# Attention and two gated layers on one core: single accumulation banks, scores by head, another split of the first layer's blocks

## The chip, the cores and the metric

One NeuronCore of one Trainium2 chip runs the whole kernel. The metric is the device time of one execution in microseconds (us). The engines are TensorE (PE in the profile, with its weight loads as PEld), VectorE (DVE), ScalarE (ACT), GpSimd (POOL) and SyncE (SP), which issues the transfers.

## The reference

```python
def _attn_ref(q, k, v, M_prev, z_prev, beta):        # B, H, S, D = 4, 8, 576, 64
    scores = scale * np.matmul(q, k.transpose(0, 1, 3, 2))
    scores = np.where(causal, -1000000000.0, scores)
    a = np.exp(scores - scores.max(-1, keepdims=True))
    a /= a.sum(-1, keepdims=True) + 1e-09
    local = np.matmul(a, v)
    q_p = phi(q)                                      # where(x > 0, x, exp(x) - 1) + 1
    mem_out = einsum('bhsd,bhde->bhse', q_p, M_prev) / (einsum('bhsd,bhd->bhs', q_p, z_prev)[..., None] + 1e-06)
    return g * mem_out + (1 - g) * local              # g: sigmoid of beta, one per head

x = attn_out.transpose(0, 2, 1, 3).reshape(2304, 512)
h = x @ w_in;  x = (h * np.tanh(softplus(h))) @ w_out     # first layer,  d_ff = 2048
h = x @ w_in2; x = (h * np.cos(h)) @ w_out2               # second layer, d_ff = 2048
```

The scores are computed for two heads at a time. Every product of the two layers is three matmuls, on the high and low halves of both operands.

## The kernel before, in words

**Attention** works on 16 pairs of heads (`pair`, four to a batch). A pair's queries and keys are turned on PE (`prep`), and its five query blocks go through three slots (`slot`; SLOTS is (3, 0), (4,), (2, 1)). In a slot, PE computes the scores of both heads into one tile of two PSUM banks (`f_sc`, L482): head 0's queries and keys lie on partitions 0 to 63 and head 1's on 64 to 127, each head has a bank of its own, and the code alternates the heads matmul by matmul. Two small bf16 matmuls per block and head add the causal mask (L495). DVE takes the negated row maximum of both heads in one instruction (L520), ACT the exponentials with their sums, one instruction a head (L536), and DVE scales the rows (L572). The scaled rows are turned on PE (`flip`, L587), copied out by ACT or DVE into PT, and multiplied with the values (`pv`, L654). The result goes to DRAM.

**The first layer** is split by the hidden dimension, 16 slices f of 128. Nine blocks of 256 tokens (`block0`, called p0 here; L759 into h, L802 into acc) use the slices 0 to 7 while attention still runs; their partial output waits in DRAM (xad). Then six blocks of 384 tokens (`late` with p = 1, called p1; L887 and L967) use the slices 8 to 15, whose weights take the SBUF of attention after its end, and add the partial output (L978). **The second layer** (`late` with p = 2, called p2; L887 and L969) is six blocks of 384 tokens with all 16 slices.

**The order** of the instructions is made by `arrange`, a list scheduler that runs while the program is built. Every task has an engine or a choice of two, a cost, a rank, the tasks it depends on, and the buffers that it takes. At each moment of the planner's own clock every free engine gets the ready task of lowest rank. Attention's ranks (100 per pair) lie under those of p0 (10000 and up), so p0 fills PE where attention has nothing ready. Before the first p0 matmul, PE gets a dummy matmul (L303) when nothing is ready. The engines then execute in this fixed order. In PSUM, p0 has one bank for h and one for acc, the scores have two tiles of two banks, and transposes and pv share two banks ("misc"); after attention's end all of it is handed to p1 and p2.

```python
    FS = (range(0, NFH), range(NFH, NF), range(0, NF))
    blocks = [(p, j) for p in range(3) for j in range(NT // TBS[p])]
    SEM, SWITCH, TABLE, WAIT = 0.1, 0.12, 1.3, 2.5
```

Of the kernel before, what the change touches and what calls it, by code (L numbers as in the profile page):

```python
# [29 lines left out]
def tile_kernel(ctx: ExitStack, tc: tile.TileContext, q, k, v, M_prev, z_prev, beta,  # L30
# [9 lines left out]
    NFH = NF // 2  # L40
# [75 lines left out]
    def decode_w(moe, f, part, op):  # L116
# [17 lines left out]
        else:  # L134
            if part == 0 and op == 3:
                wt[moe, f] = (wpa if f < NFH else pools["wpb"]).tile([P, 2, 2, 512], F32R, tag=f"w{f}", name=f"w{moe}_{f}")
# [15 lines left out]
    class Buf:  # L152
        def __init__(self, cls):
            self.cls, self.users, self.n = cls, [], made.get(cls, 0)
            made[cls] = self.n + 1

    class Task:
        __slots__ = ("eng", "cost", "fn", "deps", "rank", "takes", "func", "mode", "lag", "end", "n", "size", "on")
# [4 lines left out]
    def add(eng, cost, fn, deps=(), rank=0.0, takes=(), uses=(), func=None, mode=0, lag=0.0, size=0):  # L163
        t = Task()
        t.eng, t.cost, t.fn, t.rank, t.takes = eng.split("/"), cost, fn, rank, list(takes)
        t.func, t.mode, t.lag, t.end, t.on, t.size = func, mode, lag, None, None, size
# [6 lines left out]
    SEM, SWITCH, TABLE, WAIT = 0.1, 0.12, 1.3, 2.5  # L173
    RATE, LAND = 160.0, 2.0

    def arrange():
# [19 lines left out]
        turn = {c: 0 for c in slots_of}  # L196
# [6 lines left out]
        def at_free(b):  # L203
            if b.cls != "misc" and b.n != turn[b.cls]:
                return None
            o = held[b.cls][turn[b.cls] % len(held[b.cls])]
# [3 lines left out]
            for u in o.users:  # L210
                if u.end is None:
                    return None
                at = max(at, u.end + SEM)
            return at

        while left:
# [7 lines left out]
            for e in ready:  # L224
# [4 lines left out]
                for r in ready[e]:  # L229
# [13 lines left out]
                    if at > now:  # L243
                        later(at)
                        continue
                    key = (t.func == "mish" != func, rank, k) if func != "mish" else (t.func != "mish", rank, k)
                    if best is None or key < best[0]:
                        best = (key, r)
                if best is None:
                    if e == "pe" and t_warm.on and not turn["h"]:  # L250
                        while done and done[0][1] < now - 3.4:
                            done.popleft()
                        if sum(y - max(x, now - 3.4) for x, y in done) < 0.75 * 3.4:
                            t = Task()
                            t.eng, t.cost, t.fn, t.on, t.end = ["pe"], 0.12, f_dummy, "pe", now + 0.12
# [12 lines left out]
                t.on, t.end = e, now + cost  # L268
                free[e] = t.end
                if e == "pe":  # L270
                    done.append((now, t.end))
# [3 lines left out]
                for b in t.takes:  # L275
                    held[b.cls][turn[b.cls] % len(held[b.cls])] = b
# [9 lines left out]
                later(t.end)  # L286
# [10 lines left out]
    def f_warm(e):  # L297
        warm["w"] = pools["h"].tile([P, 2, T0], F32, tag="h", name="warm")
# [3 lines left out]
    def f_dummy(e):  # L302
        nc.tensor.matmul(warm["w"][:, 0], ident_b, warm["z"], start=True, stop=True)  # L303

    t_warm = add("dve", 0.2, f_warm)
# [35 lines left out]
    def misc(name):  # L341
        return pools["misc"].tile([P, 512], F32, tag="m", name=name)
# [787 lines left out]
```

## Time and profile before

| | us |
|---|---|
| median of 3 runs (lowest to highest) | 1081.99 (1081.27 to 1083.91) |
| span of the profiled execution | 1080.1 |
| PE busy | 1053.2 (98%), 6938 matmuls |
| PEld busy | 938.7 (87%) |
| DVE busy | 761.6 (71%) |
| ACT busy | 570.1 (53%) |
| mean granted TensorE clock | 1.000 |

The profiled execution's own time is not listed apart from the three runs; its span, from the first to the last instruction, is 1.2 us under the fastest run and 1.9 us under the median. The page says of each engine how long it was busy, in which slices of the span, and which chain of work ended last. That chain is 88% PE, 7% DVE and 3% ACT. A matmul's recorded duration (a mean of 337 ns on 384 columns) holds its way through the array; how often one can start is read from the distance between two starts.

### The profile page before, as it was taken

How to read it: one execution, taken by the hardware profiler on the slowest of the kernel's cores; microseconds unless marked ns; L12 is line 12 of the kernel's file. 1: busy time of each engine (PE TensorE's matmuls, PEld its weight loads, DVE VectorE, ACT ScalarE, POOL GpSimd, SP SyncE). 2: the span in 40 equal slices, each digit the busy share in tenths (PEclk: the TensorE clock that was granted, in tenths of full speed). 3: DMA queues.
4: the chain of work that ended last, by engine and by line, in shares of the span. 5: the costliest groups of instructions: out<-in, count | busy, mean ns of one | idle time of the engine just before them, and what ended most of it. 6: DMA issues, size and time to landing. Idle time of an engine off the chain costs nothing.

```text
span 1080.1 us, 17930 instructions
## 1 busy us (share of the span) xinstructions
PE 1053.2 (98%) x6938; PEld 938.7 (87%) x6938; DVE 761.6 (71%) x1694; ACT 570.1 (53%) x1279; POOL 3.8 (0%) x19
## 2 busy tenths in 40 slices
PE   8898999999999999999999999999999999999998
PEld 5666778788877899989999999998999999999997
DVE  6999997886787568757552228887666676766664
ACT  4676675676676443433323234766555555555544
POOL 1000000000000000000000000000000000000000
PEclk9999999999999999999999999999999999999999
DMA  6455423222322165446352216211000010000000
GB/s 165 114 132 161 113 55 103 69 70 67 100 69 59 44 204 156 137 135 205 102 183 88 89 59 187 79 38 59 1 30 30 1 59 2 30 30 1 30 1 30
DMA packets 112853, 88.73 MB, mean 82 GB/s; under 512 B 65792, under 2 KB 103680, under 8 KB 112768
## 3 DMA queue, kind: packets, MB, share of 16 engines
q1 hardware_dynamic: 112768, 87.58, 27.1%
q8 instruction: 55, 0.90, 0.3%
q14 instruction: 30, 0.25, 0.1%
HBM read 68.69 MB, written 18.87 MB: 81 GB/s over the span
## 4 chain that ended last, share of the span: by engine, by line
PE 88%; DVE 7%; ACT 3%; issue 1%; POOL 0%; ACTq 0%; POOLq 0%; DVEq 0%
PE h L887 28%; PE acc L969 18%; PE acc L967 9%; PE h L759 9%; PE acc L802 9%; PE pv L654 5%; PE t L587 4%; PE s L491 3%; DVE nm L520 2%; DVE p L572 1%; PE warm L303 1%; ACT p L536 1%; PE ptq L400 1%; ACT PT L315 1%; PE ptk L400 1%
## 5 line engine op out<-in xcount | busy, mean ns | idle before, releaser
L887 PE MATMUL h<-x,w 128*128 128x384 f32 x1728 | 345.0, 337 | 1.6 <-ACT g L903 1.6
L887 PEld LDWEIGHTS h<-x,w 128*128 128x128 f32 x1728 | 307.4, 188 | 17.2 <-ACT g L903 1.8
L969 PE MATMUL acc<-w,G 128*128 128x512 f32 x864 | 228.4, 393 | 0.0
L969 PEld LDWEIGHTS acc<-w,G 128*128 128x128 f32 x864 | 160.0, 188 | 22.1
L954 DVE TENSOR_TENSOR G<-g,G 128x384 fp32r<-128x384 f32 x144 | 79.8, 555 | 100.2 <-ACT G L315 99.6
L759 PE MATMUL h<-x,w 128*128 128x256 f32 x864 | 127.7, 288 | 4.6 <-DVE g L317 4.2
L802 PE MATMUL acc<-G,w 128*128 128x256 f32 x864 | 129.7, 289 | 1.1 <-ACT o L315 0.7
L759 PEld LDWEIGHTS h<-x,w 128*128 128x128 f32 x864 | 111.4, 191 | 9.0 <-DVE g L317 5.2
L315 ACT ACTIVATE G<-g 128x384 fp32r<-128x384 f32 (+1 forms) x152 | 81.2, 535 | 66.6 <-DVE g L938 35.8
L802 PEld LDWEIGHTS acc<-G,w 128*128 128x128 f32 x864 | 111.9, 191 | 4.0 <-ACT o L315 1.4
L967 PE MATMUL acc<-G,w 128*128 128x384 f32 x576 | 112.6, 336 | 0.0
L536 ACT ACTIVATE p<-s,nm 128x64 f32<-128x64 f32 (+4 forms) x160 | 81.3, 515 | 40.0 <-DVE nm L520 26.2
L967 PEld LDWEIGHTS acc<-G,w 128*128 128x128 f32 x576 | 100.9, 188 | 0.0
L931 ACT ACTIVATE n<-n 128x384 f32<-128x384 f32 x96 | 49.9, 521 | 63.5 <-DVE n L927 63.5
L903 ACT ACTIVATE g<-h 128x384 f32<-128x384 f32 x48 | 23.4, 491 | 113.1 <-PE h L887 112.2
L587 PE MATMUL t<-ident,p 128*128 128x128 f32 (+1 forms) x480 | 73.7, 277 | 7.8 <-ACT PT L315 3.7
L520 DVE TENSOR_REDUCE nm<-s 128x2 f32<-128x1024 f32 (+4 forms) x80 | 62.2, 790 | 23.5 <-PE s L495 16.4
L915 DVE TENSOR_SCALAR u<-hs 128x384 f32<-128x384 f32 x96 | 34.5, 359 | 54.6 <-ACT hs L315 51.9
L938 DVE TENSOR_TENSOR g<-n,hs 128x384 f32<-128x384 f32 x96 | 53.2, 555 | 26.3 <-ACT n L934 26.2
L587 PEld LDWEIGHTS t<-ident,p 128*128 128x128 f32 (+1 forms) x480 | 52.3, 140 | 18.5 <-ACT PT L315 7.8
L315 ACT ACTIVATE hs<-h 128x384 f32<-128x384 f32 x96 | 47.0, 490 | 39.3 <-PE h L887 36.6
L315 ACT ACTIVATE PT<-t 128x256 f32<-128x256 f32 (+3 forms) x97 | 43.4, 466 | 42.0 <-PE t L587 41.5
(91 smaller groups left out, 1243.6 us busy)
## 6 DMA issues: line engine op xcount, KB each, us to landing
raw<-in_moe_w_in_dram SPq DMA_DIRECT2D x32, 512.0 KB, 4.3
raw<-in_moe_w_out_dram SPq DMA_DIRECT2D x32, 512.0 KB, 3.8
k<-in_k_dram SPq DMA_DIRECT2D x32, 144.0 KB, 2.8
x1d<-xs SPq DMA_DIRECT2D x32, 144.0 KB, 2.1
xad<-o SPq DMA_DIRECT2D x9, 512.0 KB, 3.7
x2d<-o SPq DMA_DIRECT2D x6, 768.0 KB, 3.6
x<-x2d SPq DMA_DIRECT2D x6, 768.0 KB, 4.2
out_dram<-o SPq DMA_DIRECT2D x18, 256.0 KB, 2.0
```

Of the source, the lines that this page charges most:

```text
L315: nc.scalar.activation(dst, src, AF.Copy, scale=1.0 if scale is None else scale)
L520: nc.vector.tensor_reduce(out=s["nm"][:, c], in_=s["sp"][i], axis=AX.X, op=ALU.max, negate=True)
L536: nc.scalar.activation(d["p", i][:, j, D + lo:D + hi], src, AF.Exp, bias=s["nm"][:, c, j:j + 1], scale=1.0, accum_out=s["sm"][:, 1 if part ...
L587: nc.tensor.transpose(ps[:, at:at + r], d["p", i][0:r, h, j * P:(j + 1) * P], ident[0:r, 0:r])
L654: nc.tensor.matmul(o[h * D:(h + 1) * D, z_ - lo:w], vt[:, h, j - 1, :] if j else d["mv"][:, h, :], PT[:, c + z_:c + hi], start=j == 0, sto ...
L759: nc.tensor.matmul(h[:, half // 2], w[:, a, 0, c * P:(c + 1) * P], x[:, e_, c, :], start=c == 0 and pi == 0, stop=c == NKC - 1 and pi == 2)
L802: nc.tensor.matmul(t[:, c], w[:, a, 1, n * P:(n + 1) * P], G[:, e_, half], start=f == 0 and pi == 0 and c == 0, stop=f == NFH - 1 and pi == 2,
L887: nc.tensor.matmul(q_["h"], w[:, a, 0, c * P:(c + 1) * P], x[:, e_, c, :], start=c == 0 and pi == 0, stop=c == NKC - 1 and pi == 2)
L938: nc.vector.tensor_tensor(out=q_["g"], in0=q_["n"], in1=q_["hs"], op=ALU.mult)
L954: ENG[e].tensor_tensor(out=q_["G"][:, 1], in0=q_["g"], in1=q_["G"][:, 0].bitcast(F32), op=ALU.subtract)
L967: nc.tensor.matmul(o, w[:, a, 1, c * P:(c + 1) * P], G[:, e_, :], start=st, stop=sp_)
L969: nc.tensor.matmul(o, G[:, a, c * P:(c + 1) * P], w[:, e_, 1, :], start=st, stop=sp_)
```

## The change

- PSUM becomes eight single banks. `arrange` hands them out by its own clock: a task takes the bank that comes free first, and a class of tiles may hold at most CAP banks that are not free yet (scores 3, transposes and pv 3, p0's h 2, acc 4, the late h 3).
- The scores are one task per head: its main matmuls and masks into one bank. The maximum is one instruction per head, and an exponential waits for the maximum of its head alone.
- p0 has six blocks of 256 tokens instead of nine. The last 768 tokens go through the first layer in two blocks of 384 with all 16 slices, first in p1, and no partial output is stored for them. The second layer takes the blocks in the same order.
- The planner's numbers change: the time between engines (SEM 0.1 to 0.035), an end later than the engine's release (TAIL, NEXT, `over`), task costs, and a bonus (KEEP) for a PE task of the same kind as the one before it; the layers' matmuls become a kind of their own (mode 3).

```diff
-    NFH = NF // 2
+    NA = 8
...
-    SEM, SWITCH, TABLE, WAIT = 0.1, 0.12, 1.3, 2.5
-    RATE, LAND = 160.0, 2.0
+    CAP = {"warm": 1, "sc": 3, "misc": 3, "h": 2, "acc": 4, "hB": 3}
+
+    def bank(b, name):
+        return pools["bank"][b.bank].tile([P, 512], F32, tag="b", name=name)
+
+    SEM, SWITCH, TABLE, WAIT = 0.035, 0.1, 1.28, 2.5
+    RATE, LAND, KEEP = 160.0, 2.0, 10000.0
+    TAIL = {"pe": 0.16, "act": 0.0, "dve": 0.0, "sp": 0.0, "host": -SEM}
+    NEXT = {"pe": 0.0, "act": -0.1, "dve": -0.09, "sp": 0.0, "host": 0.0}
...
+            if b.cls in CAP:
+                best, n = None, 0
+                for k, o in enumerate(banks):
+                    f = clear(o)
+                    if o is not None and o.cls == b.cls and (f is None or f > now):
+                        n += 1
+                    if f is not None and (best is None or f < best):
+                        best, b.bank = f, k
+                return None if n >= CAP[b.cls] else best
+            return clear(held[b.cls][turn[b.cls] % len(held[b.cls])])
...
+                    if e == "pe" and t.mode == mode:
+                        rank -= KEEP
...
-            def f_sc(e):
-                s["sc"] = pools["sc"].tile([P, 2, 512], F32, tag="s", name=f"s{m}_{x}")
+            def f_sc(e, j):
+                s["sc", j] = o = bank(bs[j], f"s{m}_{x}_{j}")
                 qT, kT = d["qT"], d["kT"]
+                pr = slice(j * D, (j + 1) * D)
                 at = 0
                 for i in SLOTS[x]:
                     s0, main = START[i], min(START[i] + ROWS[i], 512)
-                    o = s["sp"][i] = s["sc"][:, :, at:at + main]
-                    for j in range(2):
-                        pr = slice(j * D, (j + 1) * D)
-                        nc.tensor.matmul(o[:, j], qT[pr, s0:s0 + P], kT[pr, 0:main], start=True, stop=False)
+                    w = s["sp", i, j] = o[:, at:at + main]
+                    nc.tensor.matmul(w, qT[pr, s0:s0 + P], kT[pr, 0:main], start=True, stop=False)
                     for y in range(2 if i else 1):
-                        for j in range(2):
-                            pr = slice(j * D, (j + 1) * D)
-                            nc.tensor.matmul(o[:, j, s0:main], pick[pr, y], mask[pr, y, 0:main - s0],
-                                             start=False, stop=y == 1 or i == 0)
+                        nc.tensor.matmul(w[:, s0:main], pick[pr, y], mask[pr, y, 0:main - s0],
+                                         start=False, stop=y == 1 or i == 0)
                     at += main
...
-            t_s = add("pe", sum(min(START[i] + ROWS[i], 512) * 4 / 2400 + 0.15 for i in SLOTS[x]), f_sc, qd + kx, S_, [bs],
-                      [B_["qT"], B_["kT"]], mode=1)
+            t_s = []
+            for j in range(2):
+                t_s.append(add("pe", sum(min(START[i] + ROWS[i], 512) * 2 / 2400 + 0.075 for i in SLOTS[x]), lambda e, j=j: f_sc(e, j),
+                               qd + kx + t_s[-1:], S_, [bs[j]], [B_["qT"], B_["kT"]], mode=1))
...
-                nc.vector.tensor_reduce(out=s["nm"][:, c], in_=s["sp"][i], axis=AX.X, op=ALU.max, negate=True)
+                nc.vector.tensor_reduce(out=s["nm"][:, c, j:j + 1], in_=s["sp", i, j], axis=AX.X, op=ALU.max, negate=True)
...
-    FS = (range(0, NFH), range(NFH, NF), range(0, NF))
-    blocks = [(p, j) for p in range(3) for j in range(NT // TBS[p])]
-    N0 = NT // T0
+    N0 = 6
+    NS = N0 * T0 // T1
+    N1 = NT // T1
+    JS = [*range(NS, N1), *range(NS)]
+    blocks = [(0, j) for j in range(N0)] + [(p, j) for p in (1, 2) for j in JS]
+
+    def FS(p, j):
+        return range(NA if p == 0 else NF) if p != 1 or j >= NS else range(NA, NF)
```

The order that results is shown at three places on PE. First, the scores of a slot (s_2 is the third slot's tile before; now s_0_0 is head 0 of the first slot and s_0_1 head 1; `x2` before is one matmul for each head). Before:

```order
L802 MATMUL acc_2_0_3251<-G_2_3_3481,w_7_2005 128x256 x6
L491 MATMUL s_2_3588<-kT_3305,qT_3333 128x320 x2
L495 LDWEIGHTS pick
L495 MATMUL s_2_3588<-mask,pick 128x128
...
L491 MATMUL s_2_3588<-kT_3305,qT_3333 128x192 x2
```

Now:

```order
L514 MATMUL s_0_0_3661<-kT_3454,qT_3511 128x64
L516 LDWEIGHTS pick
L516 MATMUL s_0_0_3661<-mask,pick 128x64
L614 MATMUL t_3_3678<-ident,p_0_3516 128x128 x4
L424 MATMUL ptk_0_3686<-ident,k_3531 128x96 x3
L614 MATMUL t_3_3693<-ident,p_0_3516 128x128 x4
L514 MATMUL s_0_1_3702<-kT_3454,qT_3511 128x448
```

A slot's matmuls stood in twos, head 0 and head 1 behind one another; now all of one head stand together, often with other work between the heads. In the whole program the tasks of two heads touch with opposite heads at 32 places.

Second, between two pairs (t is a tile of transposed rows of one pair; acc and h are p0's). Before:

```order
L802 MATMUL acc_2_1_3607<-G_2_1_3108,w_3_1262 128x256 x6
L587 MATMUL t_0_3690<-ident,p_0_3521 128x64 x2
L802 MATMUL acc_2_1_3607<-G_2_2_3479,w_4_1445 128x256 x6
L587 MATMUL t_4_3703<-ident,p_1_3524 128x128 x4
L587 MATMUL t_4_3709<-ident,p_1_3524 128x128 x4
L802 MATMUL acc_2_1_3607<-G_2_2_3479,w_5_1578 128x256 x6
L587 MATMUL t_4_3726<-ident,p_1_3524 128x128 x2
L587 MATMUL t_2_3730<-ident,p_2_3635 128x128 x3
```

Now:

```order
L614 MATMUL t_0_3715<-ident,p_0_3516 128x64 x2
L614 MATMUL t_4_3720<-ident,p_1_3580 128x128 x4
L614 MATMUL t_4_3729<-ident,p_1_3580 128x128 x4
L614 MATMUL t_4_3737<-ident,p_1_3580 128x128 x2
L838 MATMUL acc_1_1_3119<-G_1_2_3142,w_5_1598 128x256 x6
L614 MATMUL t_2_3753<-ident,p_2_3616 128x128 x3
```

Fewer of p0's matmuls stand between attention's, and PE changes less often between kinds of work (from scores to transposes, pv, layers or dummies and back): 266 times in the whole order, 350 before.

Third, the end of attention, the last pv (the number behind acc or h is p0's block). Before:

```order
L654 MATMUL pv_1_4944<-PT_4836,v_4469 64x256 x2
L654 MATMUL pv_1_4944<-PT_4836,v_4469 64x128 x2
L802 MATMUL acc_4_1_4920<-G_4_1_4651,w_2_1037 128x256 x6
L759 MATMUL h_5_0_4664<-x_4018,w_1_693 128x256 x6
L802 MATMUL acc_4_1_4920<-G_4_1_4651,w_3_1262 128x256 x6
```

Now:

```order
L681 MATMUL pv_1_4450<-PT_4310,v_4065 64x256 x2
L681 MATMUL pv_1_4450<-PT_4310,v_4065 64x128 x2
L838 MATMUL acc_2_0_4440<-G_2_0_4420,w_1_627 128x256 x6
L792 MATMUL h_2_3_4408<-x_2657,w_7_1960 128x256 x6
L838 MATMUL acc_2_0_4440<-G_2_1_4422,w_2_1012 128x256 x6
```

Ahead of the last pv stood 942 of p0's 1728 matmuls; now 474 of 1152 do. Ahead of the seventh pair's last pv it was 180, and is now 234. The dummies are 137 instead of 218.

## Rows read from the trace of the kernel before

**Rows 1.** Busy time by stretch; columns: stretch, length, engine busy (instructions), clock, DMA.

```profile
core 0: us, PE busy (x) PEld busy (x) DVE busy (x) ACT busy (x) POOL busy (x), PEclk, DMA share, GB/s
0.00:165.00 165.00, 147.95 (x1234) 108.87 (x1235) 149.58 (x383) 106.23 (x312) 3.84 (x19) 1.00 0.47 123
165.00:373.10 208.10, 205.28 (x1753) 170.55 (x1752) 158.10 (x411) 132.23 (x354) 0.00 (x0) 1.00 0.27 70
373.10:480.80 107.70, 104.22 (x822) 101.38 (x822) 69.45 (x122) 41.09 (x64) 0.00 (x0) 1.00 0.47 149
480.80:681.00 200.20, 200.19 (x1152) 200.20 (x1153) 104.29 (x185) 69.78 (x129) 0.00 (x0) 1.00 0.42 140
681.00:1080.10 399.10, 395.59 (x1981) 357.70 (x1980) 280.15 (x596) 220.82 (x424) 0.00 (x0) 1.00 0.07 24
```

**Rows 2.** Timeline of PE around the seventh pair's end, and behind the last pv.

```profile
162.97 1.79 PE L654 MATMUL pv<-PT,v 128*64 128x288 f32 x16
...
371.75 1.30 PE L654 MATMUL pv<-PT,v 128*64 128x288 f32 x12
372.99 0.98 PE L802 MATMUL acc<-G,w 128*128 128x256 f32 x6
373.80 0.88 PE L759 MATMUL h<-x,w 128*128 128x256 f32 x6
374.52 0.88 PE L802 MATMUL acc<-G,w 128*128 128x256 f32 x6
```

**Rows 3.** Groups of instructions by line on PE, 0 to 165 us.

```profile
L303 PE MATMUL warm<-zeros,ident_b 128*128 128x256 bf16 x218 | 31.1, 285 | 2.0 <-DVE zeros L300 2.0
```

**Rows 4.** The chain that ended last, one piece: start, us, what.

```profile
7.12 1.31 PE warm L303 x12
```

**Rows 5.** Timeline of PE, a window of 0.07 us at the start of a pair's scores.

```profile
257.23 0.65 PE L491 MATMUL s<-kT,qT 64*128 64x448 f32 x2
```

**Rows 6.** Timeline of PE, the three slots of that pair's scores and what follows.

```profile
257.23 1.02 PE L491 MATMUL s<-kT,qT 64*128 64x448 f32 x4
258.08 0.28 PE L495 MATMUL s<-mask,pick 64*128 64x128 bf16 x4
258.20 0.39 PE L491 MATMUL s<-kT,qT 64*128 64x64 f32 x4
258.42 0.20 PE L495 MATMUL s<-mask,pick 64*128 64x64 bf16 x2
258.45 1.11 PE L491 MATMUL s<-kT,qT 64*128 64x512 f32 x4
259.39 0.23 PE L495 MATMUL s<-mask,pick 64*128 64x64 bf16 x4
259.55 0.47 PE L400 MATMUL ptk<-ident,k 96*128 96x96 f32 x3
...
265.17 0.81 PE L491 MATMUL s<-kT,qT 64*128 64x320 f32 x4
...
266.51 0.98 PE L802 MATMUL acc<-G,w 128*128 128x256 f32 x6
```

**Rows 7.** Timeline of PE, p0 between transposes.

```profile
246.00 0.98 PE L759 MATMUL h<-x,w 128*128 128x256 f32 x6
246.83 1.03 PE L587 MATMUL t<-ident,p 128*128 128x128 f32 x8
247.62 0.96 PE L759 MATMUL h<-x,w 128*128 128x256 f32 x6
248.41 0.78 PE L587 MATMUL t<-ident,p 128*128 128x128 f32 x5
```

**Rows 8.** Groups by line and shape on DVE: the maxima of the longest and shortest blocks.

```profile
L520 DVE TENSOR_REDUCE nm<-s 128x2 f32<-128x1024 f32 x16 | 19.4, 1210 | 0.9 <-PE s L495 0.9
...
L520 DVE TENSOR_REDUCE nm<-s 128x2 f32<-128x128 f32 x16 | 4.6, 287 | 6.0 <-ACT p L536 6.0
```

More of the change, by code (lines that the diff above doesn't have):

```diff
@@ L200, in arrange, with clear @@
         now, order, left = 0.0, [], len(tasks)
[L203 to L206, printed above, removed]
+        def clear(o):
             if o is None:
@@ L267, in arrange @@
                     cost, mode = cost + (SWITCH if t.mode != mode else 0.0), t.mode
-                t.on, t.end = e, now + cost
-                free[e] = t.end
+                t.on, t.end = e, now + cost + TAIL[e]
+                free[e] = now + cost + NEXT[e] + (t.over if e != "pe" else 0.0)
                 if e == "pe":
-                    done.append((now, t.end))
+                    done.append((now, free[e]))
                 if t.size:
@@ L285, in arrange @@
                         put(d)
-                later(t.end)
+                later(free[e])
                 if e == "host":
@@ L302, in f_dummy @@
     def f_dummy(e):
[L303 to L305 removed]
+        nc.tensor.matmul(warm["w"][:, 0:T0], ident_b, warm["z"], start=True, stop=True)
+    b_warm = Buf("warm")
+    t_warm = add("dve", 0.2, f_warm, takes=[b_warm])
     def run(order):
@@ L807, in second @@
                                   R + (15 + 10 * u if side == 0 else 45 + u), [ba[side]] if f == 0 else [],
-                                  [bg[u], w_buf[0, f]] + ([ba[side]] if f else []))
+                                  [bg[u], w_buf[0, f]] + ([ba[side]] if f else []), mode=3)
         for u in range(NU):
             unit(u)
-            if u % 2:
-                second(u - 1, 0)
-                second(u, 0)
+            if u % 2 or u == NU - 1:
+                for v_ in range(u - u % 2, u + 1):
+                    second(v_, 0)
         bo = Buf("o")
@@ L827, in block0 @@
         return lasts[1]
-    seq = [(bi, p, j, f) for bi, (p, j) in enumerate(blocks) if p for f in FS[p]]
     RL = 30000.0
@@ L858, in late @@
             sp.append(add("dve", 0.95, f_lo, [a], R0 - 60, [], [bx]))
-        ba = [Buf(f"acc{c}") for c in range(na)]
+        ba = [Buf("acc") for c in range(na)]
         bo = Buf("o2")
-        if p == 1:
+        part_ = p == 1 and j < NS
+        if part_:
             def f_xa(e):
@@ L1059, in tile_kernel @@
         pair(m)
-    for i in range(2 * NFH):
-        weight(i, 200.0 + 30.0 * i)
+    for i in range(2 * NA):
+        weight(i, W0 + W1 * i)
     prev = None
```

149 lines of the change are left out of this document (81 added, 68 removed).

## The prediction

> **What bounds the kernel now.** I read first the busy time by stretch [rows 1], since the share over the whole span mixes stages. PE is the limit from 165 us on: 205.3 of 208.1 us busy until attention's end, 104.2 of 107.7 in the rest of p0, 200.19 of 200.20 in p1, 395.6 of 399.1 in p2. DVE is busy 158.1 of 208.1 us at the same time in the second half of attention, so it has room. Only the first 165 us are different: PE is busy for 147.95 us and 31.1 of these are dummies [rows 3], so 48 us hold no work of PE's, while DVE is busy for 149.6. That stretch goes at the pace of the chain through DVE and ACT. Then I looked for two marks in the timeline [rows 2]: the seventh pair's pv ends at about 165 us, and the last pv at 373.1, behind which p0 has PE to itself. Last I went into one pair's scores [rows 5, 6], because the change rewrites them.
>
> **Rates.** Behind attention six matmuls of 256 columns start every 0.72 us [rows 2], 0.12 us each. In p1 1152 matmuls of 384 columns fill 200.2 us [rows 1], 0.1738 each. A dummy costs 1.31/12 = 0.109 [rows 4].
>
> **Behind attention.** p0 had 786 matmuls left there and now has 678 (1728 - 942 and 1152 - 474): 108 fewer at 0.12 are 13.0 us less. p1 gets 2 blocks of 16 slices and 4 of 8, so 64 steps of 24 matmuls instead of 48: 384 more at 0.1738 are 66.7 us more. p2 is the same work. So what follows the last pv grows from 707.0 us (1080.1 - 373.1) to 760.7. The additions and reads of partial output that fall away for two blocks lie on DVE and on transfers beside a PE that is busy without a gap in p1 [rows 1], and I cost them at nothing; if weights for slices 8 to 15 came late, PE would wait there, but they have 678 matmuls, 81 us, of p0 as cover. So **the last pv must come 53.7 us earlier, at 319.4 us, for the change to break even.**
>
> **Attention, what it saves.** From the seventh pair's end to the last pv the order before holds 762 matmuls of p0 (942 - 180), and now 240 (474 - 234): 522 at 0.12 are 62.6 us off PE. Six matmuls between transposes take 0.83 and 0.79 us from start to start instead of 0.72 [rows 7], so such an insertion costs about 0.09 on top. PE changes its kind of work 84 times less often, 66 of them in this stretch, which is 33 insertions fewer: 3.0 us at 0.09, and 6.6 if each single change costs 0.1. I take 4.5.
>
> **Attention, what it adds.** At the start of a pair's scores two fp32 matmuls of 448 columns begin within a window of 0.07 us [rows 5], one of each head, and only these two; each head's matmul is two passes, and the four are through in 0.85 us, when the masks start (257.23 to 258.08, [rows 6]). The heads lie on different partitions, so they run side by side on two halves of the array's rows. Now a head's matmuls and masks stand alone. A head's passes and masks follow one another as before, on its own half of the rows, and nothing runs on the other half: I expect one head's task to take as long as both did. The three slots took 1.22, 1.10 and 1.34 us from start to start (257.23 to 258.45, to 259.55, and 265.17 to 266.51, [rows 6]), 3.66 a pair. So a pair pays up to 3.66 us more. Where tasks of opposite heads touch (32 places), I allow 0.1 us of overlap at the seam, 3 us in all, and take 3.5 us a pair: 31.5 us for the nine pairs from the eighth on. Bounds: 0, if nothing is lost, and 9 x 3.66 = 32.9. The planner books half of both heads' time for each head, so it doesn't see this.
>
> The Trainium skill ("TensorE: Matmul & The Clock Gate", Part 3: Packing small matmuls) states that matmuls on different row groups run concurrently, starting about 4 ns apart, when they follow one another. By that rule the split in itself doubles PE's time for the scores, against the planner's booking; the trace agrees, with both starts inside 70 ns.
>
> **The first seven pairs.** PE's real work there was 147.95 - 31.1 = 116.9 us. 54 matmuls of p0 more (234 - 180) add 6.5, and seven pairs at 3.5 add 24.5: 147.9. The 137 dummies, all in this part, add 15 at 0.109. That is 163 us, plus the 2 us of waiting before the first dummy [rows 3] and some of the wait for the first pair's chain, which is there as before. DVE gets five maxima more a pair. By the longest and the shortest [rows 8] a column costs 1.03 ns ((1210 - 287)/896) and a maximum 0.155 us besides, so five more are 0.8 us, 5.4 in seven pairs; they are hidden where PE is the later one now, and the upper bound holds them. So this part ends at 172 us instead of 165; bounds 165 (all of it goes into the 48 us) and 182.
>
> **The sum.** The last pv comes at 172 + 208.1 - 62.6 - 4.5 + 31.5 = 344.5 us, 25 us past break-even, and the span is 344.5 + 760.7 = 1105.2. The runs' median lies 1.9 us over the span of the profile, so I predict **1107 us**. DVE doesn't set it: from the seventh pair on it was busy 158.1 us, loses its share of p0, gains 9 x 0.8 = 7.2 for the maxima, and the stretch is now 172.5 us long. ACT has still more room (132.2).
>
> **Rivals.**
> *The seams hide the neighbour.* If PE lets a head's first matmul start while the other head's task is still running, each of the 32 touching places hides up to the shorter task, about 1.05 us: 33 us in all, 9/16 of it, 18.6, after the seventh pair, and 3 before. That gives 1107 - 21.6 = 1085. For it: the two heads do run side by side today. Against it: between touching tasks stand the first task's masks, on its own half of the rows, which must be passed. The Trainium skill (same page and part) says that matmuls start and end strictly in program order; no run here shows it, and by it this rival falls away.
> *The split costs nothing: faster.* If a head alone took half of what both take, the planner's booking would be right: 31.5 us less after the seventh pair and 3 before, 1107 - 34.5 = 1072. It decides from the score's price: below about 0.9 us a pair instead of 3.5 the kernel is faster than before. For it: the bookings were otherwise brought near to the records. Against it: a head's own passes are one behind the other, 0.85 us for two passes of 448 columns [rows 6], and nothing in a head's task became shorter. Then DVE, at 150 us or so for these pairs, would also come close to PE and could give back up to 9 of the gain (1072 to 1081).
> *PE loses its clock.* The granted clock is 1.00 in every stretch [rows 1]. From the eighth to the fourteenth pair there is now little of p0 between attention's small matmuls, and the dummies are over. If PE is held to the lower of its two levels for half of four pairs, at about 18 us of PE each, it costs 36 us: 1143. Nothing in the trace speaks for it but the dummies' being there in the first part, where the clock held too.
>
> **How the numbers follow.** The forecast gets 0.70, with 1095 to 1121 from its bounds (the first part 7 us less or 10 more, the insertions, a few us of waits in the second part). The seams get 0.12 (1079 to 1092), the free split 0.13 (1066 to 1081), the clock 0.05. The range 1080 to 1121 leaves out most of the free split, the clock, and little else. Faster or slower by over 0.3% means under 1078.7 or over 1085.2, about what a measurement of this kernel can tell from no change. Faster: most of the free split, 0.12. Same: the rest of it and half of the seams, 0.08. Slower: 0.80.
>
> **What would show it.** In the changed kernel's profile the scores' matmuls of one head should stand alone: no two starts inside 0.07 us, and about 7.0 us of PE a pair for the scores. The last pv should come at 344 us, p1's matmuls should stand alone from about 435, p1 should last some 267 us and p2 399, as before. PE should stay over 97% busy from the seventh pair to the last pv, with DVE lower. The forecast is wrong if two heads' tasks are seen side by side, if the last pv comes before 325 us, or if DVE is what PE waits for there.

## The result and the profile after

| | before | after |
|---|---|---|
| median (lowest to highest), us | 1082.33 (1081.27 to 1083.91) | 1094.13 (1093.64 to 1094.40) |
| span of the profiled execution, us | 1080.1 | 1092.6 |
| matmuls | 6938 | 6665 |

The changed kernel takes 1.0111 times as long [1.0097, 1.0125]: slower, as forecast, but by 12 us and not by 25. It lies inside the range, nearer to the rival of the seams (1085) than to the forecast (1107).

From the page of the changed kernel, busy time by engine and the granted clock:

```profile
PE 1073.4 (98%) x6665; PEld 953.1 (87%) x6665; DVE 713.9 (65%) x1668; ACT 595.7 (55%) x1363; POOL 3.9 (0%) x19
...
PEclk9999999999999999999999999999999999999999
```

PE holds 273 matmuls fewer and is busy 20 us longer. At the prediction's rates the new counts alone would make it some 11 us less (576 at 0.12 and 81 dummies at 0.109 fewer, 384 at 0.1738 more). So some of its work became dearer, and the granted clock is not the reason.

Busy time by stretch of the changed kernel (columns as in [rows 1]), cut at the seventh pair's end, the last pv, p1's start alone and p1's end:

```profile
0.00:175.30 175.30, 162.83 (x1216) 122.78 (x1216) 154.08 (x428) 107.96 (x317) 3.87 (x19) 0.99 0.47 121
175.30:334.70 159.40, 158.48 (x1222) 118.27 (x1220) 136.45 (x413) 107.11 (x327) 0.00 (x0) 1.00 0.29 73
334.70:426.00 91.30, 90.76 (x728) 90.12 (x729) 62.71 (x108) 35.44 (x56) 0.00 (x0) 1.00 0.52 167
426.00:693.00 267.00, 267.00 (x1538) 267.00 (x1537) 112.92 (x199) 91.68 (x171) 0.00 (x0) 1.00 0.30 98
693.00:1092.60 399.60, 394.36 (x1968) 354.92 (x1966) 247.71 (x523) 253.48 (x495) 0.00 (x0) 1.00 0.07 24
```

Against [rows 1] the first stretch grew by 10 us, the second fell from 208 to 159 us, and what follows the last pv grew from 707 to 758. PE is busy for 158.5 of 159.4 us in the second stretch while DVE has 23 us of room: PE sets the pace there, as forecast. p1 is 267 us without a gap, p2 is as long as before.

The timeline of PE at the last pv, the answer to [rows 2]:

```profile
332.91 1.79 PE L681 MATMUL pv<-PT,v 128*64 128x288 f32 x16
334.63 0.98 PE L838 MATMUL acc<-G,w 128*128 128x256 f32 x6
335.45 0.88 PE L792 MATMUL h<-x,w 128*128 128x256 f32 x6
```

Attention ends at 334.6 us: 38 us earlier than before, 15 too late to break even at 319.4, and 10 earlier than forecast.

The timeline of PE over one pair's scores, the answer to [rows 6]:

```profile
288.98 1.02 PE L514 MATMUL s<-kT,qT 64*128 64x448 f32 x2
...
290.29 1.20 PE L614 MATMUL t<-ident,p 128*128 128x128 f32 x9
291.42 1.02 PE L514 MATMUL s<-kT,qT 64*128 64x448 f32 x2
292.27 0.27 PE L516 MATMUL s<-mask,pick 64*128 64x128 bf16 x2
292.34 0.69 PE L514 MATMUL s<-kT,qT 64*128 64x512 f32 x3
292.61 0.19 PE L516 MATMUL s<-mask,pick 64*128 64x64 bf16 x1
292.87 0.59 PE L514 MATMUL s<-kT,qT 64*128 64x512 f32 x1
293.30 0.22 PE L516 MATMUL s<-mask,pick 64*128 64x64 bf16 x2
293.45 0.98 PE L614 MATMUL t<-ident,p 128*128 128x128 f32 x7
...
296.50 1.12 PE L514 MATMUL s<-kT,qT 64*128 64x512 f32 x4
...
297.85 0.71 PE L681 MATMUL pv<-PT,mv 128*64 128x288 f32 x4
...
303.35 0.80 PE L514 MATMUL s<-kT,qT 64*128 64x320 f32 x2
...
304.69 0.47 PE L424 MATMUL ptk<-ident,k 96*128 96x96 f32 x3
```

The tasks that stand alone cost what the forecast said: head 0's first slot takes 1.31 us (288.98 to 290.29) where both heads took 1.22, and a head's third slot 1.34 us (303.35 to 304.69), as both heads did. But where two tasks touch they cost less than their sum. Head 1's first slot and head 0's second take 2.03 us together (291.42 to 293.45). Head 1's second slot and head 0's third take 1.35 us together (296.50 to 297.85), so one of them is free. The pair's scores are 1.31 + 2.03 + 1.35 + 1.34 = 6.03 us, against 3.66 before and 7.16 by the forecast. Summed over the second stretch (each matmul of scores and masks from its own start to the next start on PE, idle left out; the eighth pair's first two slots lie ahead of the cut) they fill 48.6 us where they filled 31.2: 17.4 us more, and not 31.5. Over all sixteen pairs they fill 95.3 us where they filled 60.0: 2.2 us a pair more, and not 3.5.

The dummies of the first stretch, the answer to [rows 3], 81 fewer:

```profile
L328 PE MATMUL warm<-zeros,ident_b 128*128 128x256 bf16 x137 | 20.4, 290 | 2.0 <-DVE zeros L325 2.0
```

The maxima by head on DVE, longest and shortest block, the answer to [rows 8]:

```profile
L543 DVE TENSOR_REDUCE nm<-s 128x1 f32<-128x512 f32 x32 | 21.7, 679 | 1.5 <-PE s L516 1.4
...
L543 DVE TENSOR_REDUCE nm<-s 128x1 f32<-128x64 f32 x32 | 6.9, 215 | 3.9 <-ACT p L563 3.7
```

### The profile page after: what moved, and what is told of

It is laid out like the page before. It is cut to its first block, busy times and chain, and to the rows that moved or that the text cites. A ratio compares the mean times of both kernels' runs of the same rounds, so it can differ in the third digit from the quotient of the medians.

```text
span 1092.6 us, 17487 instructions
## 1 busy us (share of the span) xinstructions
PE 1073.4 (98%) x6665; PEld 953.1 (87%) x6665; DVE 713.9 (65%) x1668; ACT 595.7 (55%) x1363; POOL 3.9 (0%) x19
## 4 chain that ended last, share of the span: by engine, by line
PE 52%; DVE 27%; ACT 16%; issue 5%; POOL 0%; ACTq 0%; DVEq 0%; POOLq 0%
PE h L923 13%; PE acc L1002 12%; PE acc L838 6%; PE s L514 6%; PE h L792 6%; DVE n L963 5%; DVE g L974 5%; ACT n L970 4%; DVE G L990 4%; ACT u L956 4%; PE t L614 4%; ACT n L967 4%; PE pv L681 3%; DVE u L951 2%; DVE nm L543 2%
## 5 line engine op out<-in xcount | busy, mean ns | idle before, releaser
L923 PE MATMUL h<-x,w 128*128 128x384 f32 x1920 | 385.9, 337 | 0.0
L1002 PE MATMUL acc<-G,w 128*128 128x384 f32 x768 | 153.4, 336 | 0.5 <-DVE G L343 0.4
L563 ACT ACTIVATE p<-s,nm 128x448 f32<-128x448 f32 (+4 forms) x160 | 82.2, 518 | 34.7 <-DVE nm L543 31.7
L514 PE MATMUL s<-kT,qT 64*128 64x192 f32 (+4 forms) x320 | 97.2, 467 | 2.5 <-ACT qT L341 1.1
L963 DVE SCALAR_TENSOR_TENSOR n<-u,hs 128x384 f32<-128x384 f32 x96 | 53.5, 558 | 48.4 <-ACT u L956 47.8
L543 DVE TENSOR_REDUCE nm<-s 128x1 f32<-128x192 f32 (+4 forms) x160 | 72.2, 467 | 17.2 <-PE s L516 12.9
L792 PE MATMUL h<-x,w 128*128 128x256 f32 x576 | 82.5, 290 | 0.9 <-DVE PT L343 0.8
L838 PE MATMUL acc<-G,w 128*128 128x256 f32 x576 | 77.4, 286 | 0.0
L956 ACT ACTIVATE u<-u,magic 128x384 f32<-128x384 f32 x86 | 52.9, 615 | 35.5 <-DVE u L951 35.3
L140 ACT ACTIVATE w<-dec 128x512 fp32r<-128x512 f32 x64 | 39.9, 629 | 56.5 <-DVE dec L131 55.3
```

The costliest lines, as they stand in the source:

```text
L514: nc.tensor.matmul(w, qT[pr, s0:s0 + P], kT[pr, 0:main], start=True, stop=False)
L543: nc.vector.tensor_reduce(out=s["nm"][:, c, j:j + 1], in_=s["sp", i, j], axis=AX.X, op=ALU.max, negate=True)
L792: nc.tensor.matmul(h[:, half // 2], w[:, a, 0, c * P:(c + 1) * P], x[:, e_, c, :], start=c == 0 and pi == 0, stop=c == NKC - 1 and pi == 2)
L838: nc.tensor.matmul(t[:, c], w[:, a, 1, n * P:(n + 1) * P], G[:, e_, half], start=f == 0 and pi == 0 and c == 0, stop=f == NA - 1 and pi == ...
L923: nc.tensor.matmul(q_["h"], w[:, a, 0, c * P:(c + 1) * P], x[:, e_, c, :], start=c == 0 and pi == 0, stop=c == NKC - 1 and pi == 2)
L956: nc.scalar.activation(q_["u"], q_["u"], AF.Identity, bias=magic)
```

## The experiments

**The theory**: PE's time for the scores decides the sign; a head's task alone costs nearly what both cost, and at a seam of opposite heads PE runs the second head beside the first, as far as its place in the order lets it. **The rivals**: the score split is not what costs (the maxima by head, the block split or the planner's numbers do); or the short seams have nothing to do with which head stands where. The first runs take the parts apart one after the other, then the seams follow. "Before" ran with each group of runs and came to 1081.8 to 1082.0 us.

### The blocks alone (e3_blocks)

The kernel before, with the new split of p0 and p1 only.

```diff
-    FS = (range(0, NFH), range(NFH, NF), range(0, NF))
-    blocks = [(p, j) for p in range(3) for j in range(NT // TBS[p])]
-    N0 = NT // T0
+    N0 = 6
+    NS = N0 * T0 // T1
+    N1 = NT // T1
+    JS = [*range(NS, N1), *range(NS)]
+    blocks = [(0, j) for j in range(N0)] + [(p, j) for p in (1, 2) for j in JS]
...
```

> The kernel before with the new blocks alone: six blocks of 256, the last 768 tokens in two blocks of 384 with all slices; its banks, scores and planner numbers stay. Theory A (the blocks only exchange 576 matmuls at 0.12 us for 384 at 0.1738, 69.1 against 66.7, behind an unchanged attention): the last pv at 373 us, span 1077 to 1080, time 1078 to 1082, no difference. Rival D (with 210 matmuls of p0 left behind attention instead of 786, the weights of slices 8 to 15 or the last tokens come late): PE waits there, 1086 to 1100.

Measured: 1078.42 us, 0.9956 [0.9939, 0.9973]. The blocks win 3.5 us, within theory A's range, and are not what costs.

### The blocks and the maxima by head (e6_maxima)

The same, with one maximum per head and exponentials that wait for their own head's; scores, pools and planner as before.

```diff
...
-                t_m = add("dve", c_dve(2 * main), f_mx, [t_s, t_m], S_ + 1, [bn] if c == 0 else [], [bs] if c == 0 else [bs, bn])
+                for j in range(2):
+                    t_m = add("dve", c_dve(main), lambda e, j=j, f=f_mx: f(e, j), [t_s, t_m], S_ + 1, [] if c or j else [bn],
+                              [bs] + ([bn] if c or j else []))
+                    got["mx", i, j] = t_m
...
```

> The kernel before with the new split of blocks (1078.4 by itself) and with the maxima taken by head, an exponential waiting for the maximum of its own head alone; scores still one task for both heads, in a tile of two banks, old pools and old planner numbers. It stands between that kernel and the one with single banks, joint scores, maxima by head and old numbers (1068.7). Theory A (the first exponential starts half a maximum earlier, so attention's chain is shorter where PE waits for it, in the first seven pairs above all): 1068 to 1073, most of the 9.7 us. Rival B (the single banks give the 9.7 us, because p0 holds two banks for h and four for acc, and transposes three instead of two): 1076 to 1081. Between 1073 and 1076 both have a share.

Measured: 1088.22 us, 1.0058 [1.0043, 1.0073]. Both theories missed: the maxima by head make this kernel 9.8 us slower than its twin with the blocks alone. The group of the maxima on DVE, the twin with the blocks alone first:

```profile
L520 DVE TENSOR_REDUCE nm<-s 128x2 f32<-128x1024 f32 (+4 forms) x80 | 62.1, 789 | 23.5 <-PE s L495 16.4 <-ACT p L536 6.9
```

and with the maxima by head:

```profile
L520 DVE TENSOR_REDUCE nm<-s 128x1 f32<-128x448 f32 (+4 forms) x160 | 73.2, 471 | 32.9 <-ACT p L540 18.9 <-PE s L495 13.5
```

Eighty more instructions cost 11.1 us of DVE, 0.69 a pair (0.8 was forecast), and DVE sits idle ahead of a maximum for 12 us more until an exponential has ended. The stretches up to the seventh pair's end and up to the last pv, blocks alone:

```profile
0.00:166.40 166.40, 149.36 (x1230) 109.73 (x1232) 149.11 (x381) 106.04 (x311) 3.85 (x19) 0.99 0.46 122
166.40:374.80 208.40, 205.59 (x1758) 170.84 (x1754) 158.56 (x412) 132.60 (x354) 0.00 (x0) 1.00 0.27 70
```

and with the maxima by head:

```profile
0.00:176.90 176.90, 156.37 (x1303) 115.74 (x1305) 155.72 (x427) 106.97 (x304) 3.86 (x19) 1.00 0.43 114
176.90:381.80 204.90, 199.50 (x1698) 163.70 (x1694) 157.09 (x452) 129.67 (x352) 0.00 (x0) 1.00 0.28 72
```

The loss is in the first seven pairs, 10.5 us, where DVE was already busy for 149 of 166 us; the second stretch is 3.5 us shorter, with 8 us less of p0 in it. PE has 3.5 us more of idle time in the first stretch and 2.6 more in the second. The planner also orders differently, so this is the price of the edit with its new order, not of 80 instructions alone.

### Single banks on top (e4_joint_oldbook)

The changed kernel, with a slot's scores as one task again (heads alternated, two single banks, CAP for scores 4) and the planner's old numbers. Against the last kernel it has the single banks more, and in the planner the layers' matmuls as a kind of their own and slightly lower costs for them and for the dummies.

```diff
...
+            bs[0].mate = bs[1]
...
-            def f_sc(e, j):
-                s["sc", j] = o = bank(bs[j], f"s{m}_{x}_{j}")
+            def f_sc(e):
+                for j in range(2):
+                    s["sc", j] = bank(bs[j], f"s{m}_{x}_{j}")
...
-    SEM, SWITCH, TABLE, WAIT = 0.035, 0.1, 1.28, 2.5
-    RATE, LAND, KEEP = 160.0, 2.0, 10000.0
+    SEM, SWITCH, TABLE, WAIT = 0.1, 0.12, 1.3, 2.5
+    RATE, LAND, KEEP = 160.0, 2.0, 0.0
...
```

> As the first run, but with the planner's numbers of before (time between engines, no bonus for the same kind, no early release, old costs of exponentials and scaling). Its order has 642 matmuls of p0 ahead of the last pv (516 in the first run) and 317 changes of PE's kind of work (237). Theory A (PE's work decides, so the numbers matter only through the changes of kind, about 0.05 to 0.1 us each, and waits): 4 to 10 us slower than the first run, 1072 to 1082. Rival B (attention's pace is DVE's and ACT's in either order): within 2 us of the first run.

Measured: 1068.73 us, 0.9871 [0.9857, 0.9886], the fastest kernel of this study: 13 us under the kernel before and 25 under the changed one. Its twin without single banks stood at 1088.2, so this step wins 19.5 us; what of it the planner's new kind and costs give was not separated from the banks. The stretches, cut at the seventh pair's end, the last pv and p0's end:

```profile
0.00:168.50 168.50, 156.46 (x1313) 119.92 (x1315) 153.84 (x430) 104.02 (x303) 3.85 (x19) 0.99 0.46 121
168.50:330.60 162.10, 161.78 (x1407) 128.29 (x1403) 149.33 (x441) 114.34 (x331) 0.00 (x0) 1.00 0.33 83
330.60:398.30 67.70, 67.70 (x551) 67.63 (x548) 48.54 (x85) 26.56 (x41) 0.00 (x0) 1.00 0.51 165
```

From the seventh pair on PE loses 0.3 us, where it lost 5.4 in the twin. The "first run" of the expectation is e1_joint below (1069.5 us). Rival B's number came true, but not its reason: PE is busy for 161.8 of 162.1 us here, so that it, and not DVE or ACT, sets the pace.

### Scores by head on top (e4_bookings)

The changed kernel with the planner's old numbers. Against the last kernel it has the score split more.

```diff
-    SEM, SWITCH, TABLE, WAIT = 0.035, 0.1, 1.28, 2.5
-    RATE, LAND, KEEP = 160.0, 2.0, 10000.0
-    TAIL = {"pe": 0.16, "act": 0.0, "dve": 0.0, "sp": 0.0, "host": -SEM}
-    NEXT = {"pe": 0.0, "act": -0.1, "dve": -0.09, "sp": 0.0, "host": 0.0}
+    SEM, SWITCH, TABLE, WAIT = 0.1, 0.12, 1.3, 2.5
+    RATE, LAND, KEEP = 160.0, 2.0, 0.0
+    TAIL = {"pe": 0.0, "act": 0.0, "dve": 0.0, "sp": 0.0, "host": -SEM}
+    NEXT = {"pe": 0.0, "act": 0.0, "dve": 0.0, "sp": 0.0, "host": 0.0}
...
```

> The changed kernel with the planner's numbers of before (SEM, SWITCH, TABLE, TAIL, NEXT, KEEP and the three task costs), scores by head as in the change. With joint scores the old numbers made 1068.7 and the new ones 1069.5. Theory A (the new numbers buy nothing by themselves, and without KEEP fewer tasks of the two heads touch, so fewer overlap): 1094 to 1102, 0 to 8 us slower than the changed kernel. Rival B (KEEP draws the heads' tasks together, and what it draws together also waits; without it the heads stand apart and PE loses up to 7.3 us a pair of scores instead of 5.8, but its idle time falls): 1088 to 1094. Rival C (the numbers do not matter with scores by head either): within 1.5 us of the changed kernel.

Measured: 1113.14 us, 1.0286 [1.0271, 1.0302]. With the old numbers the score split costs 44.4 us, and the new numbers win 19.0 of it back, more than any of the theories gave. The same stretches:

```profile
0.00:184.80 184.80, 173.87 (x1287) 128.83 (x1287) 156.50 (x430) 106.67 (x313) 3.86 (x19) 0.99 0.44 115
184.80:372.70 187.90, 187.77 (x1380) 140.49 (x1374) 145.42 (x425) 114.32 (x331) 0.00 (x0) 1.00 0.27 67
372.70:444.00 71.30, 71.30 (x581) 71.24 (x578) 51.88 (x91) 29.20 (x43) 0.00 (x0) 1.00 0.52 168
```

p0 ends 45.7 us later than in the last kernel. Counted from start to start, the scores and masks take 106.4 us here and 60.9 there: the whole loss is PE's time for the scores, 2.84 us a pair. In the changed kernel they take 95.3: 11 us of what the new numbers win is at the seams, for its order has 32 of them and this one 16. The dummies, which only stand in for waiting, fill 28.4 us here and 18.3 there. Which of the numbers does it, KEEP or the costs, was not taken apart.

### The changed kernel with joint scores (e1_joint)

One score task for both heads, heads alternated, in the changed kernel with its new numbers (and CAP for scores 4, since a task takes two banks).

```diff
...
-            t_s = []
-            for j in range(2):
-                t_s.append(add("pe", sum(min(START[i] + ROWS[i], 512) * 2 / 2400 + 0.075 for i in SLOTS[x]), lambda e, j=j: f_sc(e, j),
-                               qd + kx + t_s[-1:], S_, [bs[j]], [B_["qT"], B_["kT"]], mode=1))
+            t_s = [add("pe", sum(min(START[i] + ROWS[i], 512) * 4 / 2400 + 0.15 for i in SLOTS[x]), f_sc,
+                       qd + kx, S_, [bs[0]], [bs[1], B_["qT"], B_["kT"]], mode=1)] * 2
```

> The changed kernel, but a slot's scores are one PE task again, the two heads alternated matmul by matmul into two single banks (scores may hold 4); maxima and exponentials stay per head, blocks and planner numbers stay. Theory A (PE's price for the split scores is what the changed kernel loses; it is 1.9 us a pair in the second part of attention and 2.5 in the first): the score tasks fall back to 3.66 us a pair, the last pv comes 20 to 26 us earlier than 334.4, near 310, and the time is 1066 to 1074 us. Rival B (PE's price is small; DVE and ACT hold attention at its pace, and the change loses elsewhere): the last pv stays above 325 us, PE shows idle time instead, and the time stays above 1083.

Measured: 1069.51 us, 0.988 [0.9866, 0.9895]. As it stands in the change, the score split costs 24.6 us (1094.1 to 1069.5); without it the change would have been faster than before. The last pv ends at 315.1 us here, 19.5 earlier than in the change, and 516 of p0's matmuls stand ahead of it instead of 474, which at 0.12 is another 5.0 us: together they make up the difference. The new numbers, at the same time, win nothing with joint scores (1068.7 with the old ones).

### Touching tasks of one head (e2_samehead)

The changed kernel with head 1 first in the second slot, so that tasks which touch are of the same head. PE's order of kinds of work is the same.

```diff
+            HO = (1, 0) if x == 1 else (0, 1)
...
-            for j in range(2):
-                t_s.append(add("pe", sum(min(START[i] + ROWS[i], 512) * 2 / 2400 + 0.075 for i in SLOTS[x]), lambda e, j=j: f_sc(e, j),
+            for j, j_ in enumerate(HO):
+                l_s.append(add("pe", sum(min(START[i] + ROWS[i], 512) * 2 / 2400 + 0.075 for i in SLOTS[x]), lambda e, j=j_: f_sc(e, j),
...
```

> The changed kernel with the heads of the second slot taken in the order 1, 0: the same tasks at the same places, but where two score tasks touch they are now of the same head (5 of the 32 touching places keep opposite heads). Theory A (PE works on the two halves of its rows as on two queues and lets a task run beside the touching one of the other head): the 14 places of 512 and 320 columns lose about 1.1 us each and the 13 of 448 and 512 columns 0.36, 20 us of PE, of which the first part hides a little: 1105 to 1115 us, near what was forecast for the change. Rival C (nothing overlaps across tasks, the split was cheaper for another reason): no difference, 1092 to 1096.

Measured: 1103.01 us, 1.019 [1.0175, 1.0206]: 8.9 us slower than the change, 2 us under theory A's range and well outside the rival's. The timeline of PE at the two seams of a pair:

```profile
298.70 1.02 PE L515 MATMUL s<-kT,qT 64*128 64x448 f32 x2
...
299.92 1.10 PE L515 MATMUL s<-kT,qT 64*128 64x512 f32 x2
...
301.01 0.98 PE L617 MATMUL t<-ident,p 128*128 128x128 f32 x7
...
303.81 1.12 PE L515 MATMUL s<-kT,qT 64*128 64x512 f32 x2
...
304.83 0.78 PE L515 MATMUL s<-kT,qT 64*128 64x320 f32 x2
...
306.14 0.71 PE L684 MATMUL pv<-PT,mv 128*64 128x288 f32 x4
```

The same two seams take 2.31 us (298.70 to 301.01) and 2.33 (303.81 to 306.14), the plain sum of their tasks, where they took 2.03 and 1.35. So the seams are cheap because the heads are opposite. Counted from start to start the scores fill 112.5 us where they filled 95.3, 17.1 more. That the time grew by only 8.9 is mostly due to the first seven pairs: they hold 8.8 of the 17.1 and end only 2.3 us later, since much of it goes into time in which PE was idle (12.5 us there in the change, 7.6 here).

### The short block first (e5_shortfirst)

The changed kernel with the 64-column block of the first slot ahead of the 448 columns.

```diff
-                at = 0
-                for i in SLOTS[x]:
+                for i in (0, 3) if x == 0 else SLOTS[x]:
                     s0, main = START[i], min(START[i] + ROWS[i], 512)
+                    at = {0: 448, 1: 320}.get(i, 0)
...
```

> The changed kernel with one thing reversed: in the first slot the 64-column block is computed ahead of the 448-column block, so that a head's score task ends with the long matmul and its masks instead of with 64 columns and their mask. PE's order of tasks is unchanged. Theory A (where two score tasks of opposite heads touch, PE can start the second head's first matmul beside the first head's, but only when few instructions of the first head are left ahead of it; in the changed kernel a 448 task that is followed by a 512 task takes 1.94 to 2.03 us with it, while tasks that end with a long matmul share 1.26 to 1.38 us): the eleven to thirteen places of 448 and then 512 fall by about 0.6 us each, and the kernel by 4 to 9 us, to 1085 to 1090. Rival B (how far two heads overlap does not hang on how many instructions stand between, but on something of the task as a whole, such as its bank or the planned gap): within 2 us of the changed kernel, 1092 to 1096. Rival C (PE overlaps nothing across tasks, and the shorter times are a chance of the records): within 1 us too, and the 512 matmuls still start where they did.

Measured: 1088.16 us, 1.0059 [1.0042, 1.0075], 6.0 us under the change, as theory A said. The timeline of PE, a task alone and then the seam:

```profile
283.12 0.43 PE L514 MATMUL s<-kT,qT 64*128 64x64 f32 x2
...
284.46 1.20 PE L613 MATMUL t<-ident,p 128*128 128x128 f32 x9
285.59 0.43 PE L514 MATMUL s<-kT,qT 64*128 64x64 f32 x2
285.86 0.19 PE L516 MATMUL s<-mask,pick 64*128 64x64 bf16 x1
285.89 1.13 PE L514 MATMUL s<-kT,qT 64*128 64x448 f32 x4
286.72 0.35 PE L516 MATMUL s<-mask,pick 64*128 64x128 bf16 x4
287.00 0.98 PE L613 MATMUL t<-ident,p 128*128 128x128 f32 x7
```

The 448 and the 512 task now take 1.41 us together (285.59 to 287.00), hardly more than the 448 task alone (1.34, 283.12 to 284.46) and 0.62 less than in the change. What a head hides at a seam hangs on how few instructions stand between the long matmuls.

### Neighbouring banks, joint maxima (e7_pairs, e8_pairs_newbook)

If maxima by head cost 9.8 us and single banks win 19.5, the two together should make a faster kernel still: a slot's two banks are neighbours, one maximum serves both heads, and the rest is as in the fastest kernel; the second run has the new planner numbers.

```diff
...
-                    b.bank, b.mate.bank = fs_[0][1], fs_[1][1]
+                    two = sorted((max(fd[k], fd[k + 1]), k) for k in range(0, 8, 2) if k in fd and k + 1 in fd)
...
+                    b.bank, b.mate.bank = two[0][1], two[0][1] + 1
...
-                    nc.vector.tensor_reduce(out=s["nm"][:, c, j:j + 1], in_=s["sp", i, j], axis=AX.X, op=ALU.max, negate=True)
+                    nc.vector.tensor_reduce(out=s["nm"][:, c], in_=s["sp", i], axis=AX.X, op=ALU.max, negate=True)
...
```

> The kernel with the new blocks, single banks handed out by the ordering pass, joint scores and old planner numbers (1068.7), but a slot's two score banks are now two neighbours, so that one maximum serves both heads again, as in the kernel before. The maxima by head cost 9.8 us on the new blocks alone (1078.4 to 1088.2), and the single banks with the maxima by head won 19.5 (1088.2 to 1068.7). Theory A (both hold independently: the maxima cost DVE time in the stretch where attention's chain sets the pace, and the banks shorten PE's waits): 1057 to 1063. Rival B (single banks only repair what the maxima by head cost, since both act on the same waits; or the need for two neighbours makes score tasks wait for a pair): 1065 to 1072.

> The same kernel with the planner's numbers of the change (SEM, SWITCH, TAIL, NEXT, KEEP and the task costs). With maxima by head and joint scores the old and the new numbers came within 0.8 us (1068.7 and 1069.5), while with scores by head the new numbers won 19.0 us (1113.1 to 1094.1). Theory A (the new numbers help only where they draw tasks of opposite heads together, which joint scores have built in): within 3 us of its twin with the old numbers. Rival B (they are nearer to the records and so order better wherever DVE is not overfull): 3 to 8 us faster than the twin.

Measured: 1075.93 us, 0.9944 [0.9929, 0.9958], and 1077.36, 0.9961 [0.9947, 0.9975]. Both theories of the first run missed. The gain does not add up: joint maxima on neighbouring banks are 7.2 us slower than maxima by head on free ones, while joint maxima were 9.8 us faster without single banks. The second run is 1.4 us from its twin, as its theory A said. The stretches of the first, cut as above:

```profile
0.00:165.00 165.00, 148.16 (x1216) 110.15 (x1216) 147.77 (x377) 101.78 (x300) 3.84 (x19) 0.98 0.46 121
165.00:324.40 159.40, 158.21 (x1367) 122.71 (x1362) 145.22 (x399) 113.37 (x339) 0.00 (x0) 1.00 0.33 84
```

Attention ends 6.2 us earlier than in the fastest kernel (324.4 and 330.6), but PE's unfilled time up to there is 18.0 us (16.84 + 1.19) against 12.4, and more of p0 is left behind it (81.6 us against 67.7). Whether it is the need for neighbours, that both heads' banks come free together, or the order that comes of it, was not separated. The new numbers again win nothing without the score split.

## Why the prediction was right and wrong

**The parts, in a row.** Each step adds one part of the change to the kernel of the line above:

| | us | step |
|---|---|---|
| before | 1081.9 | |
| the blocks | 1078.4 | -3.5 |
| maxima by head | 1088.2 | +9.8 |
| single banks (and the layers as a kind) | 1068.7 | -19.5 |
| scores by head | 1113.1 | +44.4 |
| the planner's numbers (the whole change) | 1094.1 | -19.0 |

**The step that failed is the price of the score split**: "I allow 0.1 us of overlap at the seam, 3 us in all, and take 3.5 us a pair: 31.5 us for the nine pairs". The first half of the argument held: a task alone takes 1.31 and 1.34 us where both heads took 1.22 and 1.34. The allowance for the seams was wrong. A seam of the second and third slot hides about 1.1 us (1.09 for a 512 task, as e2_samehead shows it, and 1.34, less 1.35), one of the first and second about 0.37 (1.31 and 1.09, less 2.03), and with 14 and 13 such places that is some 20 us and not 3. So the split added 17.4 us to the second stretch, 14.1 less than forecast (some 2 of these only because the eighth pair's first two slots lie ahead of the cut), and that is more than the whole miss of the span (1105.2 against 1092.6). The runs say the same: the forecast without its split (31.5 + 3) is 1072, and the changed kernel with joint scores ran in 1069.5; the split itself was put at 34.5 us and measured 24.6.

**The rival of the seams** had the mechanism and carried 0.12. Its objection, that the first task's masks must be passed, was the mistake: they are overtaken, and two heads' tasks are seen side by side, which the prediction had named as a sign of its being wrong. Nor was it so that "no run here shows it": [rows 5] already spoke against a strict order. There two first passes of 448 columns, one of each head, start within 0.07 us, while a head's own second pass follows its first by 0.48 us (291.42 and 291.90 in the changed kernel). In the code head 0's matmul stands ahead of head 1's, so if the two passes of a matmul stand together in the program, head 1's first pass started ahead of head 0's second. The rival's size was too big (33 us hidden), since a task that ends with a short block lets little through. I should have priced a seam by both bounds, 0 and 1.05 us at each of the 32 places, since no row showed its size, and taken a value between.

**What held.** Behind attention: 760.7 forecast, 758 measured; p1 267 us, p2 399.6. In the second stretch p0 and the insertions were to save 67.1; p0 filled 69.0 us less, attention's other work 4.3 more, and PE's idle time fell by 1.4: 66.1. PE was the bound there and DVE was not. The free split (1072) is refuted by the tasks that stand alone. The clock kept its upper level of 2.4 GHz, granted at 0.99 to 1.00 in every stretch, also where the dummies had ended and p0 was thin.

**The first seven pairs** ended at 175.3 us and not at 172, although the split added only 17.9 us there (46.7 from start to start, 28.7 before) and not 24.5. Two things stood against it. First, the dummies: the step "147.95 - 31.1" took them off by their recorded busy time, but their starts fill only 28.8 us, since the records of neighbours overlap; and the 137 that are left fill 18.3 us and not 15. With that, PE's work there comes to 162.4 us, by luck what the sum had (163). Second, PE is idle for 12.9 us, and not for 9. The maxima's 5.4 us on DVE, which I costed at nothing "where PE is the later one now", are a likely part of it, though no run shows it for the whole change: with the blocks alone the maxima by head cost 10.5 us in this stretch, where DVE is busy for 149 of 166.

**What cancelled.** I gave the single banks no term at all and the planner's numbers only the 4.5 us of fewer insertions; on their own steps they won 19.5 and 19.0. These steps are not terms of my sum, since each was measured with the parts above it in place: the numbers win 19.0 with scores by head and nothing with joint ones, and maxima by head cost 9.8 with fixed banks and win 7.2 against joint ones on neighbours. The order of the new kernel, from which I counted p0's matmuls ahead of the last pv, already held much of what they do. I take this to be why the sum without the split still came out within 3 us, but no run shows it.

## What to carry to other kernels

When work on two halves of the array's rows is split into tasks, count a task alone at the full time of the pair, and then look at each seam: the second task is nearly free if the long matmuls of the two halves stand within a few matmuls of one another (here up to three between), costs most of its time if more stand between, and all of it if both tasks use the same half. Alternate the halves in the code rather than leave it to an ordering pass that books each at half; here that is worth 24.6 us in the whole change and 44.4 under the old numbers. A change with several parts deserves a ladder of runs, since a maximum or a bank that wins in one setting loses in the next.

## What the runs showed of the hardware

PE lets a matmul on one half of the rows start ahead of matmuls on the other half that stand before it in the program. The timeline of the changed kernel in a window of 0.06 us at the first seam:

```profile
291.90 0.54 PE L514 MATMUL s<-kT,qT 64*128 64x448 f32 x1
292.27 0.27 PE L516 MATMUL s<-mask,pick 64*128 64x128 bf16 x2
292.34 0.69 PE L514 MATMUL s<-kT,qT 64*128 64x512 f32 x1
```

In program order come two passes of 448 columns, two masks, two passes of 64 columns, a mask, and then the 512 columns of the other head. The 512 start at 292.34, with the second mask, while the two passes of 64 columns and their mask have not begun: three matmuls are overtaken. The window at the second seam:

```profile
296.50 0.69 PE L514 MATMUL s<-kT,qT 64*128 64x512 f32 x2
```

Here two first passes, 512 columns of head 1 and 320 of head 0, begin inside 0.04 us, and again three stand between, the second pass of 512 and its two masks. With the short block first the 512 begin with the first pass of the 448 (285.89 in both cases), past its second pass and two masks. In none of these three seams is a fourth overtaken, and in the first of them a fourth would have let the 512 start earlier. Over the whole trace of the changed kernel it is the same: at each of the 32 seams the second head's first pass starts ahead of exactly three matmuls of the first, and in the trace of e2_samehead, where tasks of one head touch, ahead of none. Whether three is a limit of PE itself was not tried further.

The Trainium skill ("TensorE: Matmul & The Clock Gate", Part 3: Packing small matmuls) states that matmuls on different row groups run concurrently; the trace agrees. It also states that matmuls start and end strictly in program order; these rows show starts out of it, and the measurement decides.
